# Top-32 masking moved into a ScalarE Prelu, in a fused attention and feed-forward kernel

## The chip, the cores and the metric

One core of a Trainium2 chip runs the whole program. The metric is device time in microseconds (us) of one execution; a median of several runs is given. In the profile PE is TensorE, PEld its weight loads, DVE is VectorE, ACT is ScalarE, POOL is GpSimd and SP is SyncE, which here only issues DMAs.

## What is computed

The reference, cut to what matters. Attention keeps, in each row of scores, those that are at least the 32nd largest; the rest get no weight. Two feed-forward blocks follow on all 2304 tokens.

```python
B, H, S, D = 4, 8, 576, 64
scores = (1 / np.sqrt(D)) * np.matmul(q, k.transpose(0, 1, 3, 2))
kth = np.partition(scores, -32, axis=-1)[..., -32:-31]
scores = np.where(scores >= kth, scores, -1e9)
attn = np.exp(scores - scores.max(-1, keepdims=True))
attn = attn / (attn.sum(-1, keepdims=True) + 1e-9)
x = np.matmul(attn, v)              # then tokens x 512
h = x @ w_in                        # 512 -> 2048
x = np.maximum(0.01 * h, h) @ w_out # 2048 -> 512
h = np.maximum(np.maximum(x @ w1, x @ w2), x @ w3)  # 512 -> 768, three times
out = h @ w2_out                    # 768 -> 512
```

## The kernel before

Products are done in float16 with every float32 operand split into a high and a low half, so each logical product is three matmuls (`three`, lines 872 to 874; in attention lines 715 and 830 to 832). The weights come in as raw 64-bit words and are turned into float32 by integer instructions on VectorE (lines 496 to 502), then measured, scaled and split on ScalarE and GpSimd.

Attention is cut into 72 steps. A step takes 128 rows of queries and two heads (or, for the 64 rows left over in a batch, 64 rows and four heads); 18 steps make a batch. In a step TensorE makes the scores (line 715), ScalarE copies them to a buffer `S` in SBUF (line 720, three such buffers of two heads each), and VectorE finds the 32 largest values of each row: four rounds of `max` (8 values at a time, line 735) with three `match_replace` between them (line 737), for each of the two heads. The values land in a small buffer `m`; column 0 is the largest, column 31 the threshold.

Meanwhile GpSimd makes the bias of the exponential from column 0 (`nb`, lines 775 and 780), and ScalarE computes the exponential of all 576 scores into `pp` (line 785, one buffer). Once the threshold is known, the mask is put on. For head 0 one VectorE instruction compares `S` with the threshold and multiplies `pp` (line 790). For head 1 VectorE writes a 0/1 mask over `S` (line 794) and GpSimd multiplies `pp` by it (line 797). ScalarE then makes the high half of `pp` (line 799), GpSimd the low half (line 801), and a transposing DMA brings both to `pt` (line 804; one buffer of `phl` and one of `pt`). TensorE multiplies by V (lines 830 to 832), VectorE takes the reciprocal of the sums (837, 838), ScalarE scales (840).

```python
op(DVE, 0.83, lambda j=j: V.scalar_tensor_tensor(
    pp()[:, j], Sb[j](), thr(j), pp()[:, j], op0=ALU.is_ge, op1=ALU.mult), ...)
...
op(DVE, 0.52, lambda j=j: V.tensor_scalar(mk(j), s2(j), thr(j), None, op0=ALU.is_ge), ...)
op(POOL, pool(S), lambda j=j: G.tensor_tensor(p2(j), p2(j), mk(j), op=ALU.mult), ...)
```

The feed-forward works on ten units of tokens: 192, 128, seven of 256, and 192. For a unit, 16 tiles of the first product (12 matmuls each) are evicted by a ScalarE Prelu (line 920), split by ScalarE (line 927) and GpSimd (line 933), and multiplied by `wo` (12 matmuls for each tile); six tiles of three products (36 matmuls each) go through a maximum on VectorE (line 1017), and are multiplied by the last weights (12 matmuls for each tile). Units 1 and on also need all the weights prepared. The tiles for a unit of the feed-forward can start when the attention steps of its tokens are done.

The order of the instructions on each engine is made before the program is built, by a planner (`Plan.run`). Every instruction is an `op` with an engine, an estimated duration, what it reads and writes, and a due time (`pr`, from `TP(i)` for step i). The planner simulates the engines and their buffers and always takes the instruction that can start first, ties going to the smaller due time. What comes out is a fixed order for each engine; on the chip each engine works in that order and waits at the instruction whose input isn't there.

Of the kernel before, what the change touches and what calls it, by code (L numbers as in the profile page):

```python
# [10 lines left out]
F16 = mybir.dt.float16  # L11
# [3 lines left out]
AF = mybir.ActivationFunctionType  # L15
ALU = mybir.AluOpType
AX = mybir.AxisListType

B, H, S, D = 4, 8, 576, 64
HP = H // 2  # L20
S2 = S // 2
# [4 lines left out]
TOPK = 32  # L26
NEG = -3.0e38
PS = 2048.0
LNPS = float(np.log(PS))
P = 128  # L30
# [172 lines left out]
def act(n, psum=False, aps=0):  # L203
    return (n * 0.833 + (70 if psum else 120) + 105 * aps) / 1000


def dve(n, fast=False):
    return (n / (2 if fast else 1) / 0.96 + 69) / 1000


def pool(n):
    return (n * 2.13 + 110) / 1000
# [7 lines left out]
def attention_moe_kernel(ctx, tc, qk, v, w_in, w_out, w123, w2o, outT):  # L220
# [9 lines left out]
    NB = {"xu": 2, "raw": 2, "hl": 1, "k2": 7, "kt": 4, "qt": 2, "vt": 4, "S": 3, "w": 1, "m": 2, "nb": 2, "pp": 1,  # L230
# [53 lines left out]
    def col(n=1, dt=F32):  # L284

        if ring[0] is not None:
            c = ring[0][0] + ring[0][1]
            ring[0][1] += n
            assert ring[0][1] <= ring[0][2]
        else:  # L290
            c = cpos[0]
            cpos[0] += n
        assert cpos[0] <= NCOL, cpos
        t = colt[:, c:c + n]
        return t if dt == F32 else t.bitcast(dt)

    def use_ring(key=None, size=0):
        if key is None:
            ring[0] = None
            return  # L300
        if key not in rings:
            rings[key] = cpos[0]
            cpos[0] += size
        ring[0] = [rings[key], 0, size]
# [54 lines left out]
    def prep_qk(b, hp, pr, fast):  # L359
        d = dr.tile([2, 2, 2, D, S], F16, name=f"dqk{b}_{hp}")  # L360
        use_ring(("qk", b % 2, hp), 11)
        bi = col(2)
        kb = ("es", b, hp)
        for a in (1, 0):
# [19 lines left out]
        es, es2 = col(), col(2)  # L384
        op(POOL, 0.32, lambda: G.tensor_tensor(es, bi[:, 0:1], bi[:, 1:2], op=ALU.mult),
           r=[(("qk", b, hp, a), "b") for a in range(2)], w=[(kb, 0)], pr=pr)
        op(POOL, 0.32, lambda: G.tensor_scalar(es2[:, 0:1], es, 0.125, None, op0=ALU.mult),
           r=[(kb, 0)], w=[(kb, 1)], pr=pr)
        op(POOL, 0.32, lambda: G.tensor_scalar(es2[:, 1:2], es, -0.125, None, op0=ALU.mult),
           r=[(kb, 0)], w=[(kb, 2)], pr=pr)  # L390
# [285 lines left out]
    EXPP = 4  # L676
# [3 lines left out]
    FM = 1  # L680

    def fused(i, j):
        return j < FM

    NBE = POOL
    NG, ND = (G, 0.34) if NBE == POOL else (V, 0.1)
    MODE = "N"
    NF0 = 0

    def fold(i):  # L690
        return "N" if i < NF0 else MODE

    def attention(i):
# [8 lines left out]
        Sp, wp, m = buf("S", [P, 2, S]), buf("w", [P, 2, 2, S2]), buf("m", [P, 2, TOPK + TOPK // 2 + 1])  # L702
# [19 lines left out]
        md = fold(i)  # L722
        KM = TOPK // 2
        if md == "N":
            thr = lambda j: m()[:, j, TOPK - 1:TOPK]
            tk = lambda j: [(m, j, 0, 3)]
            wj = lambda j: wp()[:, j].rearrange("p x s -> p (x s)")
            for g in range(7):
                for j in range(2):
                    r = g // 2  # L730
                    mc = lambda j=j, r=r: m()[:, j, 8 * r:8 * r + 8]
                    src = (lambda j=j: Sb[j]()) if g < 2 else (lambda j=j: wj(j))
                    rd = [(Sp, j)] if g < 2 else [(wp, j, 0)]
                    if g % 2 == 0:
                        op(DVE, dve(S) * 1.03, lambda mc=mc, src=src: V.max(mc(), src()), r=rd, w=[(m, j, 0, r)], pr=pd)  # L735
                    else:
                        op(DVE, dve(S) * 1.03 + 0.06, lambda mc=mc, src=src, j=j: V.match_replace(  # L737
                            out=wj(j), in_to_replace=mc(), in_values=src(), imm_value=NEG),
                           r=[(m, j, 0, r)] + rd, w=[(wp, j, 0)], pr=pd)
        else:  # L740
            thr = lambda j: m()[:, j, TOPK + KM:]
            tk = lambda j: [(m, j, 2)]
            for x, o in ((0, ALU.max), (1, ALU.min)):
                E, eng, du = (G, POOL, 1.32) if md == "P" else (V, DVE, 0.83)
                op(eng, du, lambda x=x, o=o, E=E: E.tensor_tensor(wp()[:, :, x], Sp()[:, :, :S2], Sp()[:, :, S2:], op=o),
                   r=[(Sp, 0), (Sp, 1)], w=[(wp, 0, x), (wp, 1, x)], pr=pd)
            for x, g in [(0, 0), (0, 1), (1, 0), (0, 2), (1, 1), (0, 3), (1, 2), (0, 4), (0, 5), (0, 6)]:
                for j in range(2):
                    r, c0 = g // 2, TOPK * x + 8 * (g // 2)
                    mc = lambda j=j, c0=c0: m()[:, j, c0:c0 + 8]  # L750
                    wx = lambda j=j, x=x: wp()[:, j, x]
                    if g % 2 == 0:
                        op(DVE, 0.375, lambda mc=mc, wx=wx: V.max(mc(), wx()), r=[(wp, j, x)], w=[(m, j, x, r)], pr=pd)
                    else:
                        op(DVE, 0.427, lambda mc=mc, wx=wx: V.match_replace(
                            out=wx(), in_to_replace=mc(), in_values=wx(), imm_value=NEG),
                           r=[(m, j, x, r)], w=[(wp, j, x)], pr=pd)
            op(DVE, 0.2, lambda: V.tensor_tensor(m()[:, :, TOPK:TOPK + KM], m()[:, :, TOPK:TOPK + KM],
                                                 m()[:, :, TOPK - 2:TOPK - 2 - KM:-1], op=ALU.min),
               r=[(m, j, 0, r) for j in range(2) for r in range(1, 4)], w=[(m, j, 1, r) for j in range(2) for r in range(2)],  # L760
               pr=pd)
            op(DVE, 0.2, lambda: V.tensor_reduce(m()[:, :, TOPK + KM], m()[:, :, TOPK - 1:TOPK + KM], axis=AX.X,
                                                 op=ALU.max),
               r=[(m, j, 0, 3) for j in range(2)] + [(m, j, 1, r) for j in range(2) for r in range(2)],
               w=[(m, j, 2) for j in range(2)], pr=pd)
        p2 = lambda j: pp()[:, j].rearrange("p (a s) -> p a s", a=2)
        s2 = lambda j: Sb[j]().rearrange("p (a s) -> p a s", a=2)
        mk = lambda j: Sb[j]().bitcast(F16).rearrange("p (a s) -> p a s", a=2)[:, :, :S // 2]
        nb = buf("nb", [P, 2])
        pp = buf("pp", [P, 2, S])  # L770
        phl = buf("phl", [P, 2, 2, S], F16)
        pt = buf("pt", [P, 2, 9, P], F16)
        if full:
            e2 = ES[b, hps[0]]
            op(NBE, ND, lambda: NG.tensor_scalar(nb(), m()[:, :, 0:1].rearrange("p a o -> p (a o)"), e2[:, 1:2],  # L775
                                                 LNPS, op0=ALU.mult, op1=ALU.add),
               r=[(m, 0, 0, 0), (m, 1, 0, 0), (("es", b, hps[0]), 2)], w=[(nb, 0), (nb, 1)], pr=pr if NBE == POOL else pd)
        else:
            for j in range(2):
                op(NBE, ND, lambda j=j: NG.tensor_scalar(nb()[:, j:j + 1], m()[:, j, 0:1], ES[b, hps[j]][:, 1:2],  # L780
                                                         LNPS, op0=ALU.mult, op1=ALU.add),
                   r=[(m, j, 0, 0), (("es", b, hps[j]), 2)], w=[(nb, j)], pr=pr if NBE == POOL else pd)
        for j in range(2):
            es = ES[b, hps[j]]
            op(ACT, act(S, aps=2), lambda j=j, es=es: A.activation(pp()[:, j], Sb[j](), AF.Exp, bias=nb()[:, j:j + 1],  # L785
                                                                  scale=es[:, 0:1]),
               r=[(Sp, j), (nb, j), (("es", b, hps[j]), 1)], w=[(pp, j)], pr=pr + EXPP)
        for j in range(2):
            if fused(i, j):
                op(DVE, 0.83, lambda j=j: V.scalar_tensor_tensor(  # L790
                    pp()[:, j], Sb[j](), thr(j), pp()[:, j], op0=ALU.is_ge, op1=ALU.mult),
                   r=tk(j) + [(Sp, j)], w=[(pp, j)], pr=pr)
            else:
                op(DVE, 0.52, lambda j=j: V.tensor_scalar(mk(j), s2(j), thr(j), None,  # L794
                                                                 op0=ALU.is_ge),
                   r=tk(j), w=[(Sp, j)], pr=pr)
                op(POOL, pool(S), lambda j=j: G.tensor_tensor(p2(j), p2(j), mk(j), op=ALU.mult),  # L797
                   r=[(Sp, j)], w=[(pp, j)], pr=pr)
            op(ACT, act(S), lambda j=j: A.activation(phl()[:, 0, j], pp()[:, j], AF.Copy),  # L799
               r=[(pp, j)], w=[(phl, 0, j)], pr=pr)  # L800
            op(POOL, pool(S), lambda j=j: G.tensor_tensor(phl()[:, 1, j], pp()[:, j], phl()[:, 0, j],  # L801
                                                         op=ALU.subtract),
               r=[(pp, j), (phl, 0, j)], w=[(phl, 1, j)], pr=pr)
# [386 lines left out]
```

## Time and profile before

| | |
|---|---|
| median of 3 runs | 1127.8 us (1126.94 to 1128.36) |
| span of the profiled execution | 1133.3 us |
| steps of attention | 72 |
| matmuls | 10292 |

The profile is of one execution of its own, whose span is given beside the runs. Busy time of an engine is the time in which at least one of its instructions was running; records that overlap count once, so the sum of the mean durations can be larger. A group of instructions is shown as line, engine, operation, out<-in by the names of the buffers, shapes, count, then busy us, mean ns of one, and idle time of the engine just before such an instruction with what ended it. A wait is put down to what came last.

### The profile page before, as it was taken

The page shows a single profiled execution, that of the slowest core. Times are in us where ns is not written, and L with a number is a line of the kernel's source. Part 1 is how long each engine was busy: PE and PEld are TensorE (multiplying, and loading weights), DVE is VectorE, ACT ScalarE, POOL GpSimd, SP SyncE. Part 2 cuts the span into 40 slices and gives each one's busy share as a digit, 9 for nine tenths or more (in the row PEclk, how much of TensorE's full clock was granted, in tenths as well). Part 3 has the DMA queues.
Part 4 walks back from the last instruction along what each step waited for, and adds up shares of the span by engine and source line. Part 5 has one row for each costly group of instructions (what it writes and reads, how often), then busy time and mean ns, then how long its engine had stood idle before and what let it go on. Part 6 is the DMA issues. An engine that isn't in the chain of part 4 may idle for free.

```text
span 1133.3 us, 27397 instructions
## 1 busy us (share of the span) xinstructions
PE 918.0 (81%) x10292; PEld 803.0 (71%) x10292; DVE 968.7 (85%) x2154; ACT 757.2 (67%) x1625; POOL 678.2 (60%) x1054
## 2 busy tenths in 40 slices
PE   2253246763798998998999999889989999899998
PEld 1142235662698987887878788778878888788998
DVE  3999999899999998999898999889989998994101
ACT  7588749886578666567877766677786666555242
POOL 5476557765558565467777645666875565455221
PEclk9999997785799999999999999999999999999999
DMA  8759356766344434345673334553763443432000
GB/s 297 233 123 269 130 152 198 189 173 118 95 101 87 97 62 78 62 86 133 154 175 81 83 67 91 78 134 73 158 150 68 90 62 60 73 63 53 25 1 16
DMA packets 268517, 125.79 MB, mean 111 GB/s; under 512 B 237408, under 2 KB 255328, under 8 KB 266336
## 3 DMA queue, kind: packets, MB, share of 16 engines
q1 hardware_dynamic: 268384, 124.04, 47.1%
q8 instruction: 81, 1.33, 0.5%
q14 instruction: 52, 0.43, 0.1%
HBM read 62.65 MB, written 14.16 MB: 68 GB/s over the span
## 4 chain that ended last, share of the span: by engine, by line
PE 36%; DMA 13%; ACT 7%; POOL 5%; DVE 4%; issue 4%; SPq 1%; POOLq 0%; ACTq 0%; DVEq 0%
DMA pt<-phl 10%; PE h L872 6%; PE h L873 6%; PE h L874 6%; PE acc L872 4%; PE acc L873 4%; PE acc L874 4%; PE s L715 2%; POOL phl L801 2%; PE h L830 2%; DVE m L735 1%; DMA raw<-in_v 1%; DVE w L737 1%; PE h L831 1%; PE h L832 1%
## 5 line engine op out<-in xcount | busy, mean ns | idle before, releaser
L735 DVE MAX8 m<-w 128x8 f32<-128x576 f32 x432 | 309.1, 747 | 0.0
L933 POOL TENSOR_TENSOR f16t<-k,f16t 128x256 f16<-128x256 f32 (+2 forms) x220 | 143.0, 652 | 195.7 <-ACT f16t L927 167.9
L737 DVE MATCH_REPLACE8 w<-m,w 128x576 f32<-128x576 f32 x288 | 212.1, 742 | 0.0
L801 POOL TENSOR_TENSOR phl<-pp,phl 128x576 f16<-128x576 f32 x144 | 184.0, 1284 | 41.0 <-ACT phl L799 39.4
L872 PE MATMUL h<-k,w 128*128 128x256 f16 (+2 forms) x720 | 190.1, 268 | 8.9 <-ACT k L1013 4.6
L873 PE MATMUL h<-k,w 128*128 128x256 f16 (+2 forms) x720 | 190.1, 268 | 2.7 <-POOL k L975 2.5
L874 PE MATMUL h<-k,w 128*128 128x256 f16 (+2 forms) x720 | 189.9, 267 | 0.0
L873 PE MATMUL acc<-f16t,wo 128*128 128x256 f16 (+2 forms) x640 | 166.6, 264 | 4.4 <-POOL f16t L933 4.4
L872 PE MATMUL acc<-f16t,wo 128*128 128x256 f16 (+2 forms) x640 | 166.7, 264 | 1.2 <-ACT f16t L927 0.6
L874 PE MATMUL acc<-f16t,wo 128*128 128x256 f16 (+2 forms) x640 | 166.6, 264 | 0.0
L872 PE MATMUL h<-xu,wi 128*128 128x256 f16 (+1 forms) x576 | 154.8, 269 | 2.2 <-DVE k L502 1.3
L873 PE MATMUL h<-xu,wi 128*128 128x256 f16 (+1 forms) x576 | 154.7, 269 | 0.0
L874 PE MATMUL h<-xu,wi 128*128 128x256 f16 (+1 forms) x576 | 154.7, 269 | 0.0
L715 PE MATMUL s<-kt,qt 128*128 128x288 f16 (+5 forms) x800 | 109.1, 287 | 55.2 <-ACT S L720 48.4
L799 ACT ACTIVATE phl<-pp 128x576 f16<-128x576 f32 x144 | 97.1, 681 | 78.2 <-DMA pt<-phl 29.1
L785 ACT ACTIVATE pp<-S,nb,colt 128x576 f32<-128x576 f32 x144 | 120.9, 861 | 14.4 <-POOL nb L775 8.0
L830 PE MATMUL h<-vt,pt 128*128 128x65 f16 (+1 forms) x800 | 92.3, 203 | 45.9 <-DMA pt<-phl 37.7
L797 POOL TENSOR_TENSOR pp<-pp,S 128x576 f32<-128x576 f32 x72 | 92.1, 1279 | 56.9 <-DVE S L794 44.1
L927 ACT ACTIVATE f16t<-k 128x256 f16<-128x256 f32 (+2 forms) x220 | 86.2, 392 | 54.5 <-DVE k L1017 51.7
L920 ACT ACTIVATE k<-h,colt 128x256 f32<-128x256 f32 (+2 forms) x160 | 71.7, 452 | 73.1 <-PE h L874 71.4
L830 PEld LDWEIGHTS <-pt 128*128 128x128 f16 (+1 forms) x800 | 81.0, 106 | 54.6 <-DMA pt<-phl 52.5
L715 PEld LDWEIGHTS <-qt 128*128 128x128 f16 (+1 forms) x800 | 64.9, 109 | 75.3 <-issue 59.8
(136 smaller groups left out, 2644.8 us busy)
## 6 DMA issues: line engine op xcount, KB each, us to landing
w<-in_w SPq DMA_DIRECT2D x18, 512.0 KB, 4.4
w<-in_w_in SPq DMA_DIRECT2D x8, 1024.0 KB, 7.0
w<-in_w_out SPq DMA_DIRECT2D x8, 1024.0 KB, 4.9
raw<-in_qk SPq DMA_DIRECT2D x24, 288.0 KB, 3.4
dqk<-hl SPq DMA_DIRECT2D x48, 144.0 KB, 2.6
kt<-dqk SPq DMA_DIRECT2D x16, 288.0 KB, 3.1
qt<-dqk SPq DMA_DIRECT2D x144, 32.0 KB, 2.2
raw<-in_v SPq DMA_DIRECT2D x12, 352.0 KB, 3.7
```

Of the source, the lines that this page charges most:

```text
L715: T.matmul(p()[osl, h, o:o + w], q()[:, hh, st, :n], k()[:, hh, kc:kc + w], start=st == 0, stop=st == 1, skip_group_check=True)
L735: op(DVE, dve(S) * 1.03, lambda mc=mc, src=src: V.max(mc(), src()), r=rd, w=[(m, j, 0, r)], pr=pd)
L737: op(DVE, dve(S) * 1.03 + 0.06, lambda mc=mc, src=src, j=j: V.match_replace(out=wj(j), in_to_replace=mc(), in_values=src(), imm_value=NEG) ...
L785: op(ACT, act(S, aps=2), lambda j=j, es=es: A.activation(pp()[:, j], Sb[j](), AF.Exp, bias=nb()[:, j:j + 1], scale=es[:, 0:1]), r=[(Sp, j) ...
L797: op(POOL, pool(S), lambda j=j: G.tensor_tensor(p2(j), p2(j), mk(j), op=ALU.mult), r=[(Sp, j)], w=[(pp, j)], pr=pr)
L799: op(ACT, act(S), lambda j=j: A.activation(phl()[:, 0, j], pp()[:, j], AF.Copy), r=[(pp, j)], w=[(phl, 0, j)], pr=pr)
L801: op(POOL, pool(S), lambda j=j: G.tensor_tensor(phl()[:, 1, j], pp()[:, j], phl()[:, 0, j], op=ALU.subtract), r=[(pp, j), (phl, 0, j)], w= ...
L830: T.matmul(o, hc, vh, start=c == 0, stop=False, skip_group_check=True)
L872: T.matmul(out, wt(0), xt(0), start=first, stop=False, skip_group_check=True)
L873: T.matmul(out, wt(0), xt(1), start=False, stop=False, skip_group_check=True)
L874: T.matmul(out, wt(1), xt(0), start=False, stop=last, skip_group_check=True)
L933: op(POOL, pool(N) + 0.044, lambda: G.tensor_tensor(hl()[:, 1, :N], g()[:, 0, :N], hl()[:, 0, :N], op=ALU.subtract), r=[(g, 0), (hl, 0)], ...
```

## The change

Two new columns are made of the top-32 buffer once the threshold is there: `nt`, minus the threshold, and `nb`, the threshold minus the maximum, which is then multiplied by the scale of the exponential and shifted by a constant as before. A ScalarE Prelu computes S + nt for each head, with slope 1 at and above zero and slope 2^107 below, into `pp`; so a score under the threshold becomes a huge negative number. The exponential then runs on `pp` in place, and its result is zero for these. The fused mask, the compare and the GpSimd product are gone. The second scale column (minus the scale) is gone, and the scale gets a lower bound. The branches for other top-32 methods, which were not in use (`MODE` was "N"), are deleted; `m` is narrower. The estimated durations of the planner for the instructions that stay, its due times and the number of buffers stay as they are, apart from the due time of the exponential, which loses an offset (`EXPP`).

```diff
+STEEP = 2.0 ** 107
...
-        use_ring(("qk", b % 2, hp), 11)
+        use_ring(("qk", b % 2, hp), 10)
...
-        es, es2 = col(), col(2)
+        es, es2 = col(), col()
...
-        op(POOL, 0.32, lambda: G.tensor_scalar(es2[:, 0:1], es, 0.125, None, op0=ALU.mult),
+        op(POOL, 0.32, lambda: G.tensor_scalar(es2, es, 0.125, 2.0 ** -54, op0=ALU.mult, op1=ALU.max),
            r=[(kb, 0)], w=[(kb, 1)], pr=pr)
-        op(POOL, 0.32, lambda: G.tensor_scalar(es2[:, 1:2], es, -0.125, None, op0=ALU.mult),
-           r=[(kb, 0)], w=[(kb, 2)], pr=pr)
...
+        nt, nb = buf("nt", [P, 2]), buf("nb", [P, 2])
...
+        c2 = lambda c: m()[:, :, c:c + 1].rearrange("p a o -> p (a o)")
+        op(POOL, 0.3, lambda: G.tensor_scalar(nt(), c2(TOPK - 1), -1.0, None, op0=ALU.mult),
+           r=tk(0) + tk(1), w=[nt], pr=pr)
+        op(POOL, 0.25, lambda: G.tensor_tensor(nb(), c2(TOPK - 1), c2(0), op=ALU.subtract),
+           r=tk(0) + tk(1) + [(m, 0, 0, 0), (m, 1, 0, 0)], w=[(nb, 0), (nb, 1)], pr=pr)
         if full:
-            e2 = ES[b, hps[0]]
-            op(NBE, ND, lambda: NG.tensor_scalar(nb(), m()[:, :, 0:1].rearrange("p a o -> p (a o)"), e2[:, 1:2],
-                                                 LNPS, op0=ALU.mult, op1=ALU.add),
-               r=[(m, 0, 0, 0), (m, 1, 0, 0), (("es", b, hps[0]), 2)], w=[(nb, 0), (nb, 1)], pr=pr if NBE == POOL else pd)
+            op(POOL, 0.34, lambda: G.tensor_scalar(nb(), nb(), ES[b, hps[0]], LNPS, op0=ALU.mult, op1=ALU.add),
+               r=[(("es", b, hps[0]), 1)], w=[(nb, 0), (nb, 1)], pr=pr)
...
         for j in range(2):
             es = ES[b, hps[j]]
-            op(ACT, act(S, aps=2), lambda j=j, es=es: A.activation(pp()[:, j], Sb[j](), AF.Exp, bias=nb()[:, j:j + 1],
-                                                                  scale=es[:, 0:1]),
-               r=[(Sp, j), (nb, j), (("es", b, hps[j]), 1)], w=[(pp, j)], pr=pr + EXPP)
-        for j in range(2):
-            if fused(i, j):
-                op(DVE, 0.83, lambda j=j: V.scalar_tensor_tensor(
-                    pp()[:, j], Sb[j](), thr(j), pp()[:, j], op0=ALU.is_ge, op1=ALU.mult),
-                   r=tk(j) + [(Sp, j)], w=[(pp, j)], pr=pr)
-            else:
-                op(DVE, 0.52, lambda j=j: V.tensor_scalar(mk(j), s2(j), thr(j), None,
-                                                                 op0=ALU.is_ge),
-                   r=tk(j), w=[(Sp, j)], pr=pr)
-                op(POOL, pool(S), lambda j=j: G.tensor_tensor(p2(j), p2(j), mk(j), op=ALU.mult),
-                   r=[(Sp, j)], w=[(pp, j)], pr=pr)
+            op(ACT, act(S, aps=1), lambda j=j: A.activation(pp()[:, j], Sb[j](), AF.Prelu, bias=nt()[:, j:j + 1],
+                                                            alpha=STEEP),
+               r=[(Sp, j), nt], w=[(pp, j)], pr=pr)
+            op(ACT, act(S, aps=2), lambda j=j, es=es: A.activation(pp()[:, j], pp()[:, j], AF.Exp,
+                                                                   bias=nb()[:, j:j + 1], scale=es),
+               r=[(nb, j), (("es", b, hps[j]), 1)], w=[(pp, j)], pr=pr)
             op(ACT, act(S), lambda j=j: A.activation(phl()[:, 0, j], pp()[:, j], AF.Copy),
                r=[(pp, j)], w=[(phl, 0, j)], pr=pr)
```

## Rows read from the trace of the kernel before

**Rows 1.** The page, part 1: span, and busy time of each engine.

```profile
span 1133.3 us, 27397 instructions
...
PE 918.0 (81%) x10292; PEld 803.0 (71%) x10292; DVE 968.7 (85%) x2154; ACT 757.2 (67%) x1625; POOL 678.2 (60%) x1054
```

**Rows 2.** Busy time by stretch: from:to, length, engines in the page's order.

```profile
0.00:300.00 300.00, 141.66 (x1341) 112.11 (x1342) 273.76 (x601) 220.23 (x411) 186.93 (x309) 0.86 0.65 183
300.00:1030.00 730.00, 680.38 (x7841) 600.29 (x7839) 682.95 (x1522) 499.91 (x1116) 461.75 (x691) 0.99 0.46 95
1030.00:1134.00 104.00, 95.96 (x1116) 90.59 (x1113) 12.01 (x32) 37.01 (x98) 29.48 (x55) 0.99 0.06 17
```

**Rows 3.** Timeline from 660 us on: start, length, instruction, out and in, count.

```profile
660.90 0.27 PE L872 MATMUL acc<-f16t,w 128*128 128x256 f16 x1
...
661.77 0.27 PE L874 MATMUL acc<-f16t,w 128*128 128x256 f16 x1
...
663.52 0.66 PE L715 MATMUL s<-kt,qt 128*128 128x64 f16 x6
...
664.01 0.27 PE L872 MATMUL h<-k,w 128*128 128x256 f16 x1
```

**Rows 4.** The fused mask (line 790) by stretch: busy time and count on VectorE.

```profile
0.00:300.00 300.00, 11.45 (x14) 0.86 0.65 183
300.00:1030.00 730.00, 48.93 (x58) 0.99 0.46 95
```

**Rows 5.** Groups of instructions on VectorE: the two masks.

```profile
L790 DVE SCALAR_TENSOR_TENSOR pp<-S,m,pp 128x576 f32<-128x576 f32 x72 | 60.4, 839 | 10.0 <-ACT pp L785 10.0
...
L794 DVE TENSOR_SCALAR S<-S,m 128x576 f16<-128x576 f32 x72 | 43.2, 600 | 1.8 <-ACT pp L785 1.8
```

**Rows 6.** Groups of instructions on ScalarE, partly with shapes kept apart.

```profile
L785 ACT ACTIVATE pp<-S,nb,colt 128x576 f32<-128x576 f32 x144 | 120.9, 861 | 14.4 <-POOL nb L775 8.0 <-POOL phl L801 6.0
L799 ACT ACTIVATE phl<-pp 128x576 f16<-128x576 f32 x144 | 97.1, 681 | 78.2 <-DMA pt<-phl 29.1 <-DVE pp L790 24.6 <-POOL pp L797 19.3
...
L920 ACT ACTIVATE k<-h,colt 128x256 f32<-128x256 f32 (+2 forms) x160 | 71.7, 452 | 73.1 <-PE h L874 71.4 <-POOL xhl L848 1.0
...
L352 ACT ACTIVATE raw<-raw,colt 128x576 f32<-128x576 f32 x24 | 18.4, 769 | 2.4 <-POOL colt L333 2.3
...
L341 ACT ACT_TABLE_LOAD x1 | 1.3, 1283 | 0.7 <-PEq L1182 0.7
```

**Rows 7.** Groups of instructions on GpSimd.

```profile
L801 POOL TENSOR_TENSOR phl<-pp,phl 128x576 f16<-128x576 f32 x144 | 184.0, 1284 | 41.0 <-ACT phl L799 39.4 <-PE s L715 0.6
...
L797 POOL TENSOR_TENSOR pp<-pp,S 128x576 f32<-128x576 f32 x72 | 92.1, 1279 | 56.9 <-DVE S L794 44.1 <-DVE colt L326 6.9 <-DVE r L837 2.1
...
L775 POOL TENSOR_SCALAR nb<-m,colt 128x2 f32<-128x2 f32 x64 | 18.1, 283 | 7.2 <-DVE m L735 1.2
...
L389 POOL TENSOR_SCALAR colt<-colt 128x1 f32<-128x1 f32 x16 | 3.6, 227 | 0.1
L385 POOL TENSOR_TENSOR colt<-colt 128x1 f32<-128x1 f32 x16 | 3.5, 218 | 0.4
```

**Rows 8.** Waits of TensorE, 300 to 1030 us: total, times, longest.

```profile
PE h L830 <- DMA pt<-phl: 24.6, 21, 4.6
PE s L715 <- ACT S L720: 6.3, 10, 1.7
```

**Rows 9.** Waits of VectorE, 300 to 1030 us.

```profile
DVE pp L790 <- ACT pp L785: 10.0, 9, 3.1
```

**Rows 10.** Waits of ScalarE, 300 to 1030 us.

```profile
ACT k L920 <- PE h L874: 55.5, 60, 3.8
...
ACT phl L799 <- DVE pp L790: 14.4, 9, 3.5
...
ACT pp L785 <- POOL nb L775: 8.0, 9, 1.5
```

**Rows 11.** Waits of GpSimd, 300 to 1030 us.

```profile
POOL pp L797 <- DVE S L794: 33.8, 21, 3.4
```

More of the change, by code (lines that the diff above doesn't have):

```diff
@@ L20 @@
 HP = H // 2
-S2 = S // 2
 NT = B * S
@@ L228, in attention_moe_kernel @@
     ctx.enter_context(tc.manual_schedule())
-    NB = {"xu": 2, "raw": 2, "hl": 1, "k2": 7, "kt": 4, "qt": 2, "vt": 4, "S": 3, "w": 1, "m": 2, "nb": 2, "pp": 1,
+    NB = {"xu": 2, "raw": 2, "hl": 1, "k2": 7, "kt": 4, "qt": 2, "vt": 4, "S": 3, "w": 1, "m": 2, "nb": 2, "nt": 2, "pp": 1,
           "phl": 1, "pt": 1, "r": 2, "xs": 1, "xhl": 1, "f16t": 4, "yj": 1,
@@ L674, in TP @@
         return TE + TS * i if i < NE else TA0 + TA * i
-    EXPP = 4
     RLAG = 2.0
@@ L679, in attention_moe_kernel @@
     NCOLD = 8
[L680 to L691, printed above, removed]
     def attention(i):
@@ L701, in attention @@
         pr -= PB
-        Sp, wp, m = buf("S", [P, 2, S]), buf("w", [P, 2, 2, S2]), buf("m", [P, 2, TOPK + TOPK // 2 + 1])
+        Sp, wp, m = buf("S", [P, 2, S]), buf("w", [P, 2, S]), buf("m", [P, 2, TOPK])
         Sb = [lambda j=j: Sp()[:, j] for j in range(2)]
@@ L721, in attention @@
                                                                p()[:, :, :288], AF.Copy), r=[p], w=[(Sp, j)], pr=pq)
[L722 to L728, printed above, removed]
-                for j in range(2):
[L730 to L735, printed above, removed]
-                    else:
[L737 to L769, printed above, removed]
+        tk = lambda j: [(m, j, 0, 3)]
+        for g in range(7):
+            for j in range(2):
+                r = g // 2
+                mc = lambda j=j, r=r: m()[:, j, 8 * r:8 * r + 8]
+                src = (lambda j=j: Sb[j]()) if g < 2 else (lambda j=j: wp()[:, j])
+                rd = [(Sp, j)] if g < 2 else [(wp, j, 0)]
+                if g % 2 == 0:
+                    op(DVE, dve(S) * 1.03, lambda mc=mc, src=src: V.max(mc(), src()), r=rd, w=[(m, j, 0, r)], pr=pd)
+                else:
+                    op(DVE, dve(S) * 1.03 + 0.06, lambda mc=mc, src=src, j=j: V.match_replace(
+                        out=wp()[:, j], in_to_replace=mc(), in_values=src(), imm_value=NEG),
+                       r=[(m, j, 0, r)] + rd, w=[(wp, j, 0)], pr=pd)
@@ L778, in attention @@
         else:
             for j in range(2):
-                op(NBE, ND, lambda j=j: NG.tensor_scalar(nb()[:, j:j + 1], m()[:, j, 0:1], ES[b, hps[j]][:, 1:2],
-                                                         LNPS, op0=ALU.mult, op1=ALU.add),
-                   r=[(m, j, 0, 0), (("es", b, hps[j]), 2)], w=[(nb, j)], pr=pr if NBE == POOL else pd)
+                op(POOL, 0.34, lambda j=j: G.tensor_scalar(nb()[:, j:j + 1], nb()[:, j:j + 1], ES[b, hps[j]], LNPS,
+                                                           op0=ALU.mult, op1=ALU.add),
+                   r=[(("es", b, hps[j]), 1)], w=[(nb, j)], pr=pr)
@@ L783, in attention @@
         for j in range(2):
             es = ES[b, hps[j]]
-            op(ACT, act(S, aps=2), lambda j=j, es=es: A.activation(pp()[:, j], Sb[j](), AF.Exp, bias=nb()[:, j:j + 1],
-                                                                  scale=es[:, 0:1]),
-               r=[(Sp, j), (nb, j), (("es", b, hps[j]), 1)], w=[(pp, j)], pr=pr + EXPP)
-        for j in range(2):
-            if fused(i, j):
-                op(DVE, 0.83, lambda j=j: V.scalar_tensor_tensor(
-                    pp()[:, j], Sb[j](), thr(j), pp()[:, j], op0=ALU.is_ge, op1=ALU.mult),
-                   r=tk(j) + [(Sp, j)], w=[(pp, j)], pr=pr)
-            else:
-                op(DVE, 0.52, lambda j=j: V.tensor_scalar(mk(j), s2(j), thr(j), None,
-                                                                 op0=ALU.is_ge),
-                   r=tk(j), w=[(Sp, j)], pr=pr)
-                op(POOL, pool(S), lambda j=j: G.tensor_tensor(p2(j), p2(j), mk(j), op=ALU.mult),
-                   r=[(Sp, j)], w=[(pp, j)], pr=pr)
+            op(ACT, act(S, aps=1), lambda j=j: A.activation(pp()[:, j], Sb[j](), AF.Prelu, bias=nt()[:, j:j + 1],
+                                                            alpha=STEEP),
+               r=[(Sp, j), nt], w=[(pp, j)], pr=pr)
```

## The prediction

> **What bounds the kernel now.** I read the busy lines of the page first [rows 1]: VectorE (DVE) 968.7 us of the 1133.3 us span, TensorE (PE) 918.0, ScalarE (ACT) 757.2, GpSimd (POOL) 678.2. An average over the span says little here, so I cut it into stretches [rows 2]. From 0 to 300 us the weights are unpacked and split beside the first attention steps: DVE is busy 273.8 us of 300, PE 141.7. From 300 to 1030 attention and feed-forward run together: DVE 683.0 of 730, PE 680.4, ACT 499.9, POOL 461.8. From 1030 on only the feed-forward of the last units is left: PE 96.0 of 104, DVE 12.0. So DVE sets the pace of the first stretch, DVE and PE look alike in the second, PE alone makes the third.
>
> How near PE is to its own limit can't be read from its busy share, since records of matmuls overlap: one lasts 0.27 us, but nine in a row start from 660.90 to 661.77 us, 0.109 us apart, for 256 columns [rows 3]. That is 0.426 ns a column. Six score matmuls of one head (1152 columns) lie between 663.52 and 664.01, 0.49 us, the same rate [rows 3].
>
> The second stretch holds 58 of the 72 attention steps, the first 14 (one fused mask instruction each [rows 4]). Eight steps make 256 tokens, one feed-forward unit. Per eight steps the stretch takes 730 / 58 x 8 = 100.7 us, and in these:
> - DVE 683.0 / 58 x 8 = 94.2 us;
> - PE, counted by starts: a unit has 16 x 12 + 16 x 12 + 18 x 12 + 6 x 12 = 672 matmuls of 256 columns, 73.2 us; a step has 2304 columns of scores and 30 attention-times-V matmuls, 1930 columns, 4234 x 0.426 ns = 1.80 us, eight of them 14.4 us; together 87.6 us (an estimate for the short matmuls, at the rate of the long ones);
> - ACT 499.9 / 58 x 8 = 69.0 us, POOL 461.8 / 58 x 8 = 63.7 us.
>
> DVE is at 93.5% of the cadence and PE at 87%: DVE is the nearer bound, PE the next, only 6.6 us behind.
>
> The Trainium skill (Perfetto Trace Analysis, Identifying the Most-Contended Engine) warns that the matmul busy share doesn't tell how near TensorE is to its roofline. By the busy share of [rows 2] PE would need 680.4 / 58 x 8 = 93.8 us, and the change could win at most 6.9 us per eight steps; by the starts of [rows 3], 13.1 us. The trace agrees with the skill, and I go by the starts.
>
> **The change part by part.** *Removed from DVE.* 72 fused masks (60.4 us) and 72 mask compares (43.2 us) [rows 5], 103.6 us in all, 1.44 us a step. 14 steps of it, 20.1 us, lie in the first stretch; 58, 83.5 us, in the second. The fused mask also waited 10.0 us for exponentials [rows 9]; that wait goes with it.
>
> *Removed from POOL.* 72 multiplications of 1.279 us, 92.1 us, and the second scale column, 16 x 0.227 us = 3.6 us [rows 7]. Their waits for the mask (33.8 us in the second stretch [rows 11]) go too.
>
> *Added to ACT.* 144 Prelus of 128x576 float32, out of and into SBUF, with one pointer operand (the bias). The nearest row has just that shape and one pointer (a scale): 0.769 us, 24 times [rows 6]. Bounds are the copy without pointers, 0.681, and the exponential with two, 0.861 [rows 6]. I take 0.769: 144 x 0.769 = 110.7 us (98 to 124), 1.54 us a step. The exponential keeps its shape and operands and I leave it at 0.861.
>
> *Added to POOL.* Per step a negation of two threshold columns and a subtraction of two columns. The negation is like the old bias instruction, 0.283 us; the subtraction like a one-column one, 0.218 [rows 7]. The old bias instruction stays, its input now the difference. So 0.50 us a step (0.4 to 0.6), 36 us; POOL ends 92.1 + 3.6 - 36 = 60 us lighter. No DMA is added or moved.
>
> *Moved.* The exponential could run during the top-32 search, since it needed only the first maximum; now Prelu and exponential both wait for the 32nd value. From the threshold on, before: fused mask 0.84, compare 0.60, POOL product 1.28, copy 0.68, POOL difference 1.28, together 4.68 us without hops. After: negation 0.28, then on ACT for two heads 2 x (0.769 + 0.861 + 0.681) = 4.62, and the last difference 1.28: 6.19 us. The probabilities reach their transpose some 1.5 us later. What is late next is the attention-times-V group on PE, which already waited 24.6 us in 21 places for that transpose [rows 8]. I cost the delay at nothing in the middle, because feed-forward matmuls of an earlier unit cover it and the planner, which is given the new instructions, places the group anew; uncovered it would be up to 58 x 1.5 = 87 us. At the end it is covered by the unit still in PE's queue.
>
> *The new wait at the head of queues.* POOL's negation waits for DVE's last maximum, and Prelu for the negation. Behind Prelu on ACT stand the evictions and float16 copies of the feed-forward, behind these POOL's differences and PE. Such waits exist already: ACT waited 14.4 us for the fused mask and 8.0 us for the bias column in the second stretch [rows 10], 0.39 us a step, POOL 33.8 us [rows 11]. I take the new wait as these were, at nothing more, and price the rest below. One old wait goes: Prelu writes the single probability buffer only after the threshold, when the step before has long left it.
>
> *Sum.* Second stretch, per eight steps after the change: DVE 94.2 - 11.5 = 82.7; ACT 69.0 + 12.3 = 81.3; POOL 63.7 - 8 x (1.28 - 0.50) = 57.5; PE 87.6. PE becomes the bound. If PE reached the 93.5% that DVE has now, the cadence would be 93.7 us and the gain 7.0 us x 58/8 = 51 us. But three engines now lie within 7 us of each other where there were two, so I take 92%: 95.2 us, gain 5.5 x 7.25 = 40 us. First stretch: at most 20.1 us, and ACT, which does the squares, scales and splits of the weights there, gains 14 x 1.54 = 21.6 us of work on 220.2 [rows 2]; I take a third, 6 us. Third stretch: PE-bound, 0. Together 46 us. Durations and sum belong to the profiled execution, whose span of 1133.3 us is 5.5 us above the median of the runs, 1127.8; I take the difference from the median: **1082 us**.
>
> **The rivals.**
> - *All of it is won.* PE runs at 96%: 91.3 us, 9.4 x 7.25 = 68 us, and the first stretch gives 18: 1042 us. For it: PE is hardly held up by ACT or POOL in the second stretch (6.3 us by score copies [rows 8]). Against: the waits for transposes remain.
> - *ACT becomes the bound.* Its share was 73% and 68% in the first two stretches [rows 2]. If a queue in order, fed by DVE, POOL and PE in turn, gets no further than 82%, the cadence is 81.3 / 0.82 = 99.1 us, gain 1.6 x 7.25 = 11 us, and nothing to 8 us before: about 1112 us. For it: six ACT instructions in a chain after each threshold. Against: ACT waited 55.5 us for feed-forward matmuls [rows 10]; it is idle because PE is late, not the other way.
> - *Slower: Prelu blocks ACT.* Prelu stands at the head of ACT while DVE, running behind plan, finishes the search; evictions stand behind it, PE runs out of PSUM banks. If PE loses 1.5 us in each of 58 steps, that is 87 us against the 46: 1169 us; from 0.8 us a step on (46 / 58) the kernel is slower. A mild case ends near 1145. For it: an idle-time filler became a chain with a deadline. Against: the present waits of that kind are half of 0.8 us a step [rows 10].
> - *Table reloads.* If Prelu and the exponential did not share ACT's function table, two loads a step at the 1.283 us of the one load in the trace [rows 6] would add 58 x 2.57 = 149 us to ACT in the second stretch, which then has 499.9 + 89 + 149 = 738 us of work in 730: about 1150 us or more. Against: the feed-forward's Prelu (160 times) and the exponential (144 times) are mixed in the kernel before, and there is one load in all [rows 6]. The Trainium skill (ScalarE: Activation LUTs, Table sets: the hidden batching unit) says that each switch to another set costs a load and lists no Prelu beside exp; the trace shows that here they need none.
>
> **How the numbers follow.** My forecast, 1063 to 1098 us: 0.52. All of it won: 0.12. ACT the bound but still faster: 0.17. No change, the two balancing within 0.2% (about 2 us, what a measurement can tell): 0.05. Prelu blocking: 0.13. Reloads: 0.01. So faster 0.81, same 0.05, slower 0.14. The range leaves out the lower half of the second case and most of the slower ones: 1052 to 1130 us.
>
> **What would show it.** Right: DVE near 865 us with no other instruction than before less the masks, ACT near 868, POOL near 618; one table load; Prelu at 0.77 us; eight steps in about 95 us and PE the fullest engine between the first unit and the end. A first stretch that is no shorter would take 6 us off the gain. Wrong: idle time of ACT before Prelu over 0.8 us a step with PE waiting for feed-forward copies; attention-times-V waiting much more than 24.6 us for the transposes; DVE waiting for score copies because its three score buffers are held longer.

## The result, and the profile after

The changed kernel takes 1089.6 us (median of four, 1084.9 to 1092.6) against 1128.1 us, a ratio of 0.9648 (95% interval 0.9618 to 0.9678; the quotient of the two medians is 0.9659). The forecast was 1082, range 1052 to 1130. The profiled execution has a span of 1089.0 us, 44.3 us under that of before.

The page of the changed kernel, its span and the busy line that answers to [rows 1]:

```profile
span 1089.0 us, 27384 instructions
...
PE 911.5 (84%) x10292; PEld 802.1 (74%) x10292; DVE 876.9 (81%) x2010; ACT 841.5 (77%) x1769; POOL 599.6 (55%) x1110
```

VectorE lost 92 us, GpSimd 79, ScalarE gained 84. The highest share is now TensorE's.

Groups of the changed kernel that answer to [rows 6] and [rows 7]; line 739 is the Prelu, 742 the exponential, 725 and 727 the negation and the subtraction on GpSimd:

```profile
L742 ACT ACTIVATE pp<-pp,nb,colt 128x576 f32<-128x576 f32 x144 | 123.2, 861 | 0.3
L739 ACT ACTIVATE pp<-S,nt 128x576 f32<-128x576 f32 x144 | 107.6, 767 | 26.4 <-POOL nt L725 16.9 <-POOL phl L747 9.2
...
L725 POOL TENSOR_SCALAR nt<-m 128x2 f32<-128x2 f32 x72 | 15.8, 219 | 26.4 <-DVE m L715 24.4 <-DVE colt L326 1.6
...
L727 POOL TENSOR_TENSOR nb<-m 128x2 f32<-128x2 f32 x72 | 14.1, 196 | 0.0
```

The cut that explains the result is another than the one of the forecast. The feed-forward of the second unit can start only when all weights are prepared; from then on TensorE has work to the end. Its first matmul is the first whose output `h` comes from `k` and `wi`. On the timelines of TensorE it stands at 319.70 us before the change:

```profile
319.70 0.22 PE L872 MATMUL h<-k,wi 128*128 128x128 f16 x1
```

and at 305.25 us after it:

```profile
305.25 0.22 PE L818 MATMUL h<-k,wi 128*128 128x128 f16 x1
```

So 14.4 us were won up to there, and 29.9 us after it: 813.6 us before, 783.7 us now. The mark is not the same point of the work, though: 16 searches have begun by then before the change, and 17 after it. Busy times of the two parts (columns as in [rows 2]), before:

```profile
0.00:320.00 320.00, 160.94 (x1588) 130.75 (x1589) 293.76 (x647) 231.87 (x436) 195.66 (x320) 0.87 0.64 178
320.00:1134.00 814.00, 757.06 (x8708) 672.24 (x8705) 674.96 (x1508) 525.28 (x1190) 482.51 (x734) 0.99 0.41 85
```

and after, with the second part cut once more where the last attention search ends:

```profile
0.00:305.00 305.00, 161.61 (x1619) 131.18 (x1620) 282.88 (x639) 253.84 (x475) 184.20 (x336) 0.74 0.66 189
305.00:956.00 651.00, 622.69 (x7273) 552.03 (x7271) 581.52 (x1341) 536.38 (x1167) 376.94 (x703) 0.99 0.46 101
956.00:1090.00 134.00, 127.22 (x1405) 118.91 (x1403) 12.49 (x33) 51.24 (x130) 38.44 (x72) 1.00 0.07 19
```

In the first part VectorE is busy 92.7% of the time after (282.9 of 305) as before (293.8 of 320, 91.8%): it bounds it in both. In the second TensorE went from 93.0% (757.1 of 814) to 95.5% (749.9 of 785). Attention ends 72 us earlier, at 956 instead of 1029 us, but what is left for TensorE alone grew from 105 to 133 us.

Waits of TensorE after 305 us in the changed kernel, against [rows 8]:

```profile
PE h L818 <- ACT k L959: 5.2, 2, 3.4
PE h L776 <- DMA pt<-phl: 4.1, 7, 1.4
...
PE s L700 <- ACT S L705: 3.4, 7, 0.9
```

The wait of attention-times-V for the transposed probabilities, 24.6 us before, is down to 4.1.

### The profile page after: what moved, and what is told of

It reads as the page before. It is cut to its first block, busy times and chain, and to the rows that moved or that the text cites. A ratio compares the mean times of both kernels' runs of the same rounds, so it can differ in the third digit from the quotient of the medians.

```text
span 1089.0 us, 27384 instructions
## 1 busy us (share of the span) xinstructions
PE 911.5 (84%) x10292; PEld 802.1 (74%) x10292; DVE 876.9 (81%) x2010; ACT 841.5 (77%) x1769; POOL 599.6 (55%) x1110
## 4 chain that ended last, share of the span: by engine, by line
PE 58%; ACT 8%; DMA 5%; DVE 5%; POOL 3%; issue 2%; SPq 1%; POOLq 0%; ACTq 0%; DVEq 0%
PE h L818 10%; PE h L819 10%; PE h L820 10%; PE acc L818 6%; PE acc L819 6%; PE acc L820 6%; PE s L700 4%; DMA pt<-phl 4%; PE h L776 2%; DVE m L715 2%; PE h L777 2%; PE h L778 2%; DVE w L717 1%; POOL phl L747 1%; ACT S L705 1%
## 5 line engine op out<-in xcount | busy, mean ns | idle before, releaser
L879 POOL TENSOR_TENSOR f16t<-k,f16t 128x256 f16<-128x256 f32 (+2 forms) x220 | 136.8, 623 | 178.2 <-ACT f16t L873 149.2
L739 ACT ACTIVATE pp<-S,nt 128x576 f32<-128x576 f32 x144 | 107.6, 767 | 26.4 <-POOL nt L725 16.9
L742 ACT ACTIVATE pp<-pp,nb,colt 128x576 f32<-128x576 f32 x144 | 123.2, 861 | 0.3
L715 DVE MAX8 m<-S 128x8 f32<-128x576 f32 x144 | 103.2, 745 | 13.3 <-ACT S L705 13.3
L819 PEld LDWEIGHTS <-w 128*128 128x128 f16 x960 | 94.9, 99 | 19.8 <-issue 11.6
```

The lines of the kernel that those rows point to most:

```text
L739: op(ACT, act(S, aps=1), lambda j=j: A.activation(pp()[:, j], Sb[j](), AF.Prelu, bias=nt()[:, j:j + 1], alpha=STEEP), r=[(Sp, j), nt], w=[ ...
L819: T.matmul(out, wt(0), xt(1), start=False, stop=False, skip_group_check=True)
L879: op(POOL, pool(N) + 0.044, lambda: G.tensor_tensor(hl()[:, 1, :N], g()[:, 0, :N], hl()[:, 0, :N], op=ALU.subtract), r=[(g, 0), (hl, 0)], ...
```

## The experiments

The theory after the trace: VectorE bounds the start, TensorE the rest, and ScalarE's 111 us are hidden. Rivals: ScalarE's added time limits; the later chain after the threshold costs; the gain is not VectorE's time but the waits between mask, product and copy. Ratios are to the kernel before, run on the same chip in the same study; a variant and the change are compared by their ratios, across studies.

**One head at a time.** Only head 1 by Prelu, in outline, against the kernel before:

```diff
+ head 1: nt, nb, Prelu, Exp in place, as in the change
- head 1: V.tensor_scalar(mk, S, thr, op0=is_ge); G.tensor_tensor(pp, pp, mk, op=mult)
  head 0: Exp early, fused mask on VectorE, as before the change
```

> One part alone: only head 1 goes through Prelu (compare on VectorE and product on GpSimd gone); head 0 keeps its fused mask on VectorE. VectorE loses 43 us of the 104, ScalarE gains 55 of the 111. Theory 'TensorE is the bound after the change': the gains of the two heads do not add up, since a part of the relief already brings VectorE under TensorE; alone some 20 to 30 us of the 38, about 1100 us. Rival 'ScalarE's added time eats the gain': half of it on ScalarE is better than all, 1080 us or less. Rival 'all of VectorE's time counts': 43/104 of 38, about 1112 us.

Measured: 1122.1 us, ratio 0.9918 (0.9894 to 0.9943). Only head 0 by Prelu, the mirror of it, in outline too:

```diff
+ head 0: nt, nb, Prelu, Exp in place
- head 0: V.scalar_tensor_tensor(pp, S, thr, pp, op0=is_ge, op1=mult)
  head 1: Exp early, compare on VectorE, product on GpSimd
```

> The other part alone: only head 0 goes through Prelu (fused mask on VectorE gone); head 1 keeps compare and GpSimd product. VectorE loses 60 us, ScalarE gains 55. Theory 'TensorE is the bound': 25 to 35 us faster than before, about 1098 us, and the two single gains together exceed 38. Rival 'ScalarE eats the gain': 1080 us or less. Rival 'all of VectorE's time counts': 60/104 of 38, about 1106 us.

Measured: 1104.2 us, ratio 0.9768 (0.9737 to 0.9798). The parts give 0.8% and 2.3%, together 3.1% of the 3.5%. They add up, and head 1 alone gave less than every expectation. That TensorE already caps the gain within these 104 us of VectorE is refuted; the cap lies further on (below). Head 1's part, which relieves GpSimd of all its products, is the smaller one. Head 0's part leaves GpSimd busier than before (716.6 us against 678.2, since each head now has small bias instructions of its own) and still wins 2.3%, so GpSimd's time is not the cause either. The busy lines with head 1 alone and with head 0 alone:

```profile
PE 912.0 (81%) x10292; PEld 799.9 (71%) x10292; DVE 935.8 (83%) x2082; ACT 799.7 (71%) x1697; POOL 645.4 (58%) x1190
...
PE 908.1 (82%) x10292; PEld 800.4 (73%) x10292; DVE 914.1 (83%) x2082; ACT 806.1 (73%) x1697; POOL 716.6 (65%) x1262
```

**ScalarE's added time.** Masks left out, nothing in their place:

```diff
-            if fused(i, j): ... V.scalar_tensor_tensor(... is_ge, mult ...)
-            else: ... V.tensor_scalar(... is_ge ...); G.tensor_tensor(... mult ...)
```

> The kernel before with both masks left out and nothing in their place (so all 576 scores get weight): VectorE 104 us and GpSimd 92 us lighter, ScalarE as before, and the exponential still early. Theory 'TensorE is the bound': what Prelu costs on ScalarE is hidden, so this is within 12 us of the changed kernel, 1078 to 1092 us. Rival 'ScalarE's added 111 us limit': 1060 us or less. Rival 'the later chain after the threshold costs': also 1060 us or less, and the next kernel stays near 1090.

Measured: 1083.1 us, ratio 0.9582 (0.9548 to 0.9617). And the change without its Prelu:

```diff
-            op(ACT, act(S, aps=1), ... A.activation(pp()[:, j], Sb[j](), AF.Prelu, ...)
+            op(ACT, act(S, aps=2), ... A.activation(pp()[:, j], Sb[j](), AF.Exp, bias=nb ...), r=[..., nt, ...])
```

> The changed kernel without Prelu: the exponential reads the scores, but still waits for the threshold (so nothing is masked). ScalarE 108 us lighter than in the changed kernel, the chain after the threshold 1.5 us shorter. Theory 'TensorE is the bound': 0 to 8 us faster than the changed kernel, 1082 to 1090 us. Rival 'ScalarE's added time limits': 1065 us or less. Rival 'the later chain costs': near the changed kernel, while the kernel without masks is much faster.

Measured: 1098.6 us, ratio 0.9716 (0.968 to 0.9753). The first is 0.7% faster than the change, the second 0.7% slower, though both have over 85 us less on ScalarE (busy 753 us each against 841.5). Less work can't cost 8 us by itself: without Prelu the second unit starts at 304.13 us, nearly as in the change, and what follows takes 796 instead of 784 us (with the masks left out it is the reverse: 314.69 and 766 us, with 18 searches begun by the start instead of 17). Each new set of durations makes the planner lay out another order, and that alone seems to move such a kernel by some 8 us; single differences of that size are not read here. What the pair does show is that no 25 us are to be had from ScalarE.

Prelu done twice turns the question round:

```diff
+            op(ACT, act(S, aps=1), lambda j=j: A.activation(pp()[:, j], Sb[j](), AF.Prelu, ...), ...)
             op(ACT, act(S, aps=1), lambda j=j: A.activation(pp()[:, j], Sb[j](), AF.Prelu, ...), ...)
```

> The changed kernel with every Prelu done twice (same input, same output): ScalarE 108 us heavier and the chain after the threshold 1.5 us longer, nothing else. Theory 'TensorE is the bound and ScalarE has slack': by the sum of busy times ScalarE would come to 81 + 12 = 93 us per eight steps against TensorE's 88, so a loss of at most 15 us, about 1095 to 1105 us. Rival 'ScalarE's time counts in full': 70 us or more, 1160 us. Rival 'ScalarE's time does not count at all': 1086 to 1093 us.

Measured: 1102.1 us, ratio 0.9766 (0.9742 to 0.9789), 1.2% or some 13 us over the change. The page of this kernel, and the first matmul of its second unit:

```profile
span 1098.9 us, 27489 instructions
...
PE 904.6 (82%) x10292; PEld 797.3 (73%) x10292; DVE 884.7 (81%) x2010; ACT 931.0 (85%) x1913; POOL 600.5 (55%) x1110
```

```profile
318.06 0.22 PE L821 MATMUL h<-k,wi 128*128 128x128 f16 x1
```

ScalarE is 89.5 us fuller, for 13 us. The second unit starts 12.8 us later, and the rest takes 780.8 us, no longer than in the change. But the mark has moved: 18 searches have begun by then, not 17, and VectorE is busy 292.8 us up to it instead of 283.1. At the beginning of step 14, a point of the same work, the second set of Prelus costs 1.1 us (the rows stand below, with the first stretch). So the start does not pay for it; what it costs comes after step 14 and is not much more than the 8 us of an order. Nearly all of twice the added work is hidden.

**VectorE's time put back.** Two compares a step that nobody uses:

```diff
+        for j in range(2):
+            op(DVE, 0.52, lambda j=j: V.tensor_scalar(mk(j), wp()[:, j].rearrange("p (a s) -> p a s", a=2),
+                                                      m()[:, j, TOPK - 1:TOPK], None, op0=ALU.is_ge),
+               r=tk(j), w=[(wp, j, 0)], pr=pr)
```

> The changed kernel with the old compare put back twice a step on VectorE, on the search's own scratch buffer, its result used by nobody: some 80 us of VectorE, no work for GpSimd or ScalarE, nothing waits for it but the next search. If the gain of the change is VectorE's time: most of it is lost again, 80/104 of 39 us, about 1119 us. If the gain is the end of the waits between mask, product and copy, or GpSimd's time: little lost, 1095 us or less.

Measured: 1118.5 us, ratio 0.9908 (0.9885 to 0.9932): of 39.7 us (3.5% of 1128) 29 are lost again. Page and first matmul of the second unit:

```profile
PE 911.7 (82%) x10292; PEld 799.1 (72%) x10292; DVE 965.3 (87%) x2154; ACT 844.3 (76%) x1769; POOL 626.2 (56%) x1110
```

```profile
319.80 0.22 PE L823 MATMUL h<-k,wi 128*128 128x128 f16 x1
```

With VectorE at 965.3 us, nearly as before the change, the second unit's start is back at 319.8 us, and the rest takes 795 us. At points of the same work: of the 27.2 us won up to step 14, 20.7 are lost again, and of the 17.1 us won after it, 5.2 (rows below). The mask's instructions and GpSimd's saved products are as in the change (GpSimd's negation takes 367 ns on average here instead of 219). So the larger part of the gain is VectorE's time, above all at the start.

What does not come back, some 10 us in the runs and 18 in the spans, VectorE's time does not explain. TensorE's wait for the transposes after the second unit's start is 9.5 us here, 24.6 before the change. Head 1 alone, which keeps the fused mask, has 19.4 us of that wait, and with VectorE 30 us lighter than here it is no faster (0.9918 against 0.9908). So the third rival, that the waits between mask, product and copy ended, fits what is left; no run separates it from the 8 us by which an order alone can differ.

**More of it taken away.** One round of the search less:

```diff
-        tk = lambda j: [(m, j, 0, 3)]
-        for g in range(7):
+        tk = lambda j: [(m, j, 0, 2)]
+        for g in range(5):
...
-c2(TOPK - 1)
+c2(23)
```

> The changed kernel with the last of the four rounds of the search left out on both heads (24 values are kept in place of 32): VectorE some 210 us lighter, all else the same. If TensorE is the bound from the second unit on: that part, 784 us in the changed kernel with 30 us of idle time on TensorE, shrinks by at most 25 us, and only the start, which VectorE bounds, gets 15 to 30 us shorter: 1040 to 1065 us. If VectorE's time still counts at the 0.37 us a us that the change had: 78 us, 1011 us.

Measured: 1061.1 us, ratio 0.9403 (0.9375 to 0.9431). Page, first matmul of the second unit, and the part after it:

```profile
PE 901.7 (85%) x10292; PEld 797.0 (75%) x10292; DVE 693.0 (65%) x1578; ACT 835.7 (79%) x1769; POOL 599.4 (57%) x1110
```

```profile
294.60 0.22 PE L818 MATMUL h<-k,wi 128*128 128x128 f16 x1
```

```profile
295.00:1059.00 764.00, 740.73 (x8630) 666.19 (x8627) 433.83 (x997) 573.16 (x1275) 406.81 (x753) 1.00 0.40 87
```

The change took 91.8 us of busy time from VectorE and won 39.7 us, 0.43 us a us. These 184 us more win 28 us, 0.15 us a us. After the start TensorE is busy 97% of the time with VectorE at 57%: here is a cap, which the theory had put too early.

**TensorE's time.** One of the three matmuls of the last product left out (240 of 10292), in the changed kernel and in the one before:

```diff
-        T.matmul(out, wt(0), xt(1), start=False, stop=False, skip_group_check=True)
-        T.matmul(out, wt(1), xt(0), start=False, stop=last, skip_group_check=True)
+        T.matmul(out, wt(0), xt(1), start=False, stop=last, skip_group_check=True)
```

> The changed kernel with one of the three matmuls of the last product left out (low half of the weights), 24 matmuls a unit, some 23 us of TensorE starts in all; the planner is given two thirds of the time. Theory 'TensorE is the bound from the second unit on': 18 to 23 us faster than the changed kernel, about 1069 us. Rivals 'ScalarE is the bound' or 'the chain after the threshold': under 8 us faster.

Measured: 1075.6 us, ratio 0.9488 (0.9453 to 0.9524), 1.6% or 18 us under the change.

> The same matmul left out in the kernel before. If VectorE was the bound there up to 1030 us, only what lies in the last stretch of 104 us counts, two units of 2.6 us and a little more: 5 to 10 us faster than before, about 1120 us. If TensorE was the bound there already: 20 us, 1107 us.

Measured: 1128.7 us, ratio 0.996 (0.9942 to 0.9977), 4.5 us. The same 23 us of matmuls (an estimate, 0.109 us for 256 columns) are worth 18 us after the change and 4.5 us before it. After the second unit's start alone it is 15.3 us (768.4 against 783.7) and 3.4 us (810.2 against 813.6). The difference is more than the 8 us of an order: the bound has moved.

**The holes at the batches.** In the changed kernel the search of attention stops twice: 45 us lie between the starts of steps 36 and 37 (counted from 0) and 25 us between 55 and 56, right behind the first steps of batches 2 and 3, not ahead of them as the expectation has it. One number is changed, first in that kernel:

```diff
-    LB = 60
+    LB = 120
```

> The changed kernel with one number changed: the queries, keys and values of batches 2 and 3 get a due time 120 instead of 60 us ahead of their first step. In the changed kernel steps 36 and 54, the first of these batches, start 45 and 26 us after the step before them instead of 10. If these holes cost only attention, while TensorE goes on with feed-forward work in stock: no change, 1086 to 1092 us. If TensorE runs out of work for them later: 10 to 18 us faster, about 1075 us.

Measured: 1076.9 us, ratio 0.9499 (0.947 to 0.9527). The stretch with the hole, in the changed kernel:

```profile
500.00:560.00 60.00, 55.14 (x593) 47.50 (x591) 29.37 (x71) 45.38 (x100) 37.44 (x88) 0.94 0.58 137
```

and with the earlier preparation:

```profile
500.00:560.00 60.00, 55.05 (x680) 47.80 (x678) 55.75 (x128) 51.83 (x111) 37.23 (x78) 1.00 0.57 116
```

VectorE is busy 55.8 us of 60 instead of 29.4, and attention is through by 918 instead of 956 us. TensorE's busy time is the same in both; the 87 additional matmuls are mostly short ones of attention. It is over the whole part after the start (304.64 us here) that it gains:

```profile
305.00:1076.00 771.00, 743.01 (x8667) 668.04 (x8664) 592.30 (x1371) 586.56 (x1294) 414.59 (x774) 1.00 0.41 88
```

Of the 14 us, 7 are idle time of TensorE (35 to 28) and 7 a lower busy time for the same matmuls (749.9 to 743.0). The holes did not cost attention alone. A part of the lower busy time goes with TensorE's granted clock: the two lines have 0.94 and 1.00, and 6% of 60 us would be 3.6 us (an estimate). In the hole TensorE was busy 6.8 us of the ten from 515 to 525; from 525 to 530 the granted clock was 0.56, near the lower of its two levels (1.2 and 2.4 GHz).

> The same number in the kernel before, where steps start 11 to 16 us apart at the batches and no hole is seen: within 5 us of before, 1123 to 1130 us, if the holes come from the faster pace alone.

Measured: 1111.5 us, ratio 0.9818 (0.9775 to 0.986). The expectation was wrong: the kernel before gains as much, 20 us. The lead was too short there too. No hole is to be seen there; what the trace has is TensorE's wait for the transposes, which falls from 24.6 to 11.9 us. With the longer lead on both sides the change is worth 0.9499 / 0.9818 = 0.9675, about what it was. The changed kernel with `LB` = 120 is the fastest version found that leaves nothing out.

## Why the prediction was right, and where it was not

**The time.** 46 us were forecast, 38.5 measured in the runs, 44.3 in the span. The mechanism held in the main: VectorE's time pays (put back, it costs 29 us of the 39.7), ScalarE hides the Prelus, TensorE becomes the bound. By the stretches of the prediction (up to the beginning of step 14, from there to the end of the last search, and what is left) the 44.3 us are 27.2 + 45.2 - 28.1, where 6 + 40 + 0 were forecast. Two terms of the sum were wrong, by 21 and 28 us in opposite directions, so that the total came so near was in part luck.

**First stretch, 6 us forecast.** It gave 27.2 us: step 14 begins at 297.84 us before and at 270.68 after. I had discounted two thirds of the 20.1 us for the work that ScalarE gains there, and this term failed. Busy times up to step 14 (columns as in [rows 2]) before, after, with the compares put back and with every Prelu done twice:

```profile
0.00:297.84 297.84, 139.50 (x1323) 110.05 (x1324) 271.60 (x596) 219.09 (x407) 184.77 (x307) 0.86 0.65 184
0.00:270.68 270.68, 131.62 (x1238) 103.10 (x1238) 250.03 (x559) 227.88 (x421) 164.33 (x302) 0.73 0.69 198
0.00:291.37 291.37, 132.09 (x1274) 104.17 (x1274) 271.46 (x594) 231.99 (x430) 173.00 (x308) 0.72 0.68 189
0.00:271.79 271.79, 128.14 (x1224) 101.74 (x1225) 249.10 (x557) 236.73 (x432) 162.84 (x302) 0.75 0.68 193
```

VectorE is idle for 20 to 26 us in each of them, and its busy time moves the end: the change took 21.6 us of it and 5.5 us of idle time, and 21.4 us put back as idle compares cost 20.7 us. A second set of Prelus costs 1.1 us. VectorE's time counts in full in this stretch and ScalarE's hardly at all. By the second unit's start 14.4 of the 27.2 us are left, since the search of one more step, over 10 us of VectorE, lies ahead of it. TensorE's clock does not decide here: up to the second unit's start it was 0.87 before and 0.74 after, and with the longer lead it is 0.88, with the start at 304.64 us as against 305.25.

**Second stretch, 40 us forecast by the cadence.** The cadence came out almost as said. The step after the first 14 (its first `max` on `S`) before:

```profile
297.84 1.39 DVE L735 MAX8 m<-S 128x8 f32<-128x576 f32 x2
```

and after, with the last `max` of the last search:

```profile
270.68 1.41 DVE L715 MAX8 m<-S 128x8 f32<-128x576 f32 x2
...
954.99 1.41 DVE L715 MAX8 m<-w 128x8 f32<-128x576 f32 x2
```

58 steps from there to the end of the last search, 956.4 us, are 685.7 us, 94.6 us per eight steps against 95.2 forecast (731 and 100.8 before).

**Third stretch, 0 forecast.** This step failed. It became 28 us longer (105 to 133). Attention's cadence is not what the end hangs on when TensorE has feed-forward work in stock: attention that is done sooner leaves more of it for the end. With the longer lead attention ends another 38 us sooner, the last stretch is 158 us, and the gain is 16.8 us. I should have summed TensorE's part from the second unit to the end, 814 us, whose idle time is the most that can be won there while its busy time stays. By its busy row before, that was 57 us, and 30 were won. It is no hard cap: with a quarter of the search left out 50 us were won, 16 of them busy time (757 to 741 us).

**TensorE's room, 13.1 us per eight steps by starts.** It was taken from the attention stretch alone, with the short matmuls at the rate of the long ones (and with 1930 columns of attention-times-V a step, where 10 x (65 + 64 + 65) is 1940; that changes nothing). Over 58/8 units 13.1 us would be 95. The cadence alone can fall nearly so far: with the longer lead it is 89.3 us (58 steps from 270.1 to 917.8 us), 11.5 under before. But the tail grows with it. The gain after the second unit's start stayed at 30 us, and even with a quarter of the search left out 764 us, with TensorE 97% busy, were the least seen, 50 us under before.

**Costs of instructions.** Prelu: 0.767 us against 0.769 from the row of equal shape. Negation and subtraction: 0.219 and 0.196 against 0.283 and 0.218. But ScalarE's total rose by 84 and not by 111 us, and VectorE's fell by 92 and not 104. I multiplied mean durations, and neighbours overlap: two exponentials of 0.861 us took 1.61 us in a row in the kernel before. (GpSimd's total fell by 79 and not 60 us; the added instructions came to 30 and not 36, and the rest was not followed up.) The Trainium skill (ScalarE: Activation LUTs, What ACT_TABLE_LOAD costs) says that ACTIVATEs back to back overlap by about 93 ns; the trace agrees roughly (2 x 0.861 - 1.61 = 0.11 us).

**The chain after the threshold, costed at nothing.** Right in that it cost nothing: attention-times-V waits 4.1 us for its transposes and not 24.6. In the other runs without the fused mask it is 4 to 13 us, in those with it 12 to 19. That less mask work between threshold and copy, and feed-forward matmuls at hand, outweigh the exponentials that moved behind it is a likely reason, not shown. I had the two chains by their durations alone and not this result.

**The rivals.** Prelu at the head of ScalarE's queue, after 305 us:

```profile
ACT pp L739 <- POOL nt L725: 10.9, 12, 2.5
```

That is 0.19 us for each of the 56 steps whose Prelus lie there, where 0.8 was the point from which it would decide. Reloads: one table load, as before. ScalarE as the bound: refuted, by the second set of Prelus, for the first stretch too. All of it won: no.

## What to carry to other kernels

When a change relieves one of two engines that are nearly level, ask which stretch of the program has which bound, and measure the gain where the other engine starts its unbroken run and where it ends, not by the pace of the relieved one. Compare at points of the same work (the beginning of the same step): a mark in the program can move because other work was put ahead of it. Work that finishes sooner on one side can come back as a longer tail on the other. A moved bound is shown by taking the same work away before and after: here 23 us of matmuls were worth 4.5 us and then 18. And where an order is laid out anew for each variant, differences under a per cent between variants say little; look for the doses that move the time by more.

## What was not expected

Nothing new of the hardware. Of the program: the lead of a batch's preparation, one number, was worth about half as much as the change in both kernels, although the kernel before shows no hole; why it pays there is not shown.
